# Retention plus bilinear feed-forward: another instruction order for the opening, query decay at the copy of the transposed queries, one state bank for both halves

## The chip, the cores and the metric

One NeuronCore of a Trainium2 chip runs the whole program. The metric is device time in microseconds (us) of one execution. Matmuls run on TensorE (PE), with separate weight loads (PEld); VectorE (DVE), ScalarE (ACT) and GpSimd (POOL) do element-wise work; SyncE (SP) mostly starts DMAs. ACT and POOL start some DMAs too. Each engine takes its instructions in the order in which they are written, and waits at an instruction whose data is not there.

## The reference, cut to what matters

```python
# q, k, v: (8 batches, 8 heads, 576 positions, 64), float32
scores = scale * q @ k.T                       # per head
Dmat   = where(rel >= 0, gamma[h] ** rel, 0)   # rel = query position - key position
att    = (scores * Dmat) @ v
x      = att.transpose(0, 2, 1, 3).reshape(4608, 512)
out    = ((x @ w_a) * (x @ w_b)) @ w_out       # 512 -> 1536 -> 512, float32
```

The decay `gamma ** (i - j)` is split into a factor of the query's position `i` (with `scale`; table `qs_o`) and one of the key's position `j` (table `vs`, multiplied into the values).

## The kernel before, in words

**The work as a whole.** The 4608 tokens are handled in feed-forward blocks of 512, 256, 256, and then 512 tokens (`blocks`). For a block, PE forms `pa = x @ w_a` and `pb = x @ w_b` for each of twelve slices F of 128 columns (lines 1398 and 1419), ACT copies `pa` to `ha` (L1412), DVE multiplies it with `pb` to `hT` (L1424), and PE forms rows `po` from `hT` and `w_out` (L933, L1445). Retention for later tokens is put between these matmuls, at moments counted in units of a 128x512 matmul: the list `todo` holds a unit and a function, and the loop at the end of the kernel calls a function at the first permitted point at or after its unit.

**The opening** is what comes before the first `pb`. It makes the retention of the first 256 tokens of batches 0 and 1, each as two steps of four heads: step 0 is batch 0 with heads 0-3, step 2 is batch 0 with heads 4-7, steps 1 and 3 are the same for batch 1. Steps 4 and 5 (batch 2, "the third") come later, inside the rows of the first feed-forward block. In a step (names and lines of the kernel before):

- loads of q, k and v, 256 KB each (`load_step`, L182): eleven of the twelve on SP's queue, step 0's k on ACT's;
- casts of q and k to bf16 (`cast_step`, L371), and values times key decay (`values_step`, L379 on ACT, L381 on DVE or POOL);
- PE transposes of q and k, four of 128x128 each (`transpose_step`, L389), copied from PSUM to `qkT` (L393);
- 16 score matmuls (`score_step`, L407), and one DVE instruction that multiplies 128x1024 scores with the causal mask (L415);
- 16 state matmuls, keys times values (L434), for the two halves a = 0, 1 of the 256 positions, into two PSUM tiles; ACT copies the first half to `state_after` in bf16 (L446, L467) and both halves to `own` and `second` (L450, L451, L469, L471), which are added later (`total_of`, L478, L481);
- two matmuls that take the state of the first half to the queries of the second (`step_states`, L504), and 16 of masked scores times values (`step_keys`, L520);
- `close_step` (L536, L541): DVE multiplies the 128x512 output in PSUM with the query decay `qs_o` and writes `x` in bf16.

The order is written out by hand (lines 1477 to 1554). Transposes and casts of steps 0, 2, 1 and 3 are started in that order; the masks are made in the order 0, 2, 1, 3. At the end stand `last_states` (states of steps 1 and 3, both halves, in one go), the outputs of 1 and 3, their closes, and then 16 matmuls of 128x256 for the first two slices of `pa` (`begin_with`, L922): slice F, contraction chunk c, token half m (m = 0 is batch 0, m = 1 is batch 1). Chunks c = 0, 1 of batch n come from its first step, c = 2, 3 from its second. `warm` issues matmuls whose result is not used (L1471), 19 in the opening.

The weights come by DMAs that POOL starts (L294, L296, L299), cast from float32 on the way: pieces of `WCOLS` slices for `w_a` and `w_b`, then three pieces of `w_out` (`wo_sb`). A one-row DMA into `gate` (L1550) makes SP's queue wait until the first piece of `w_out` has arrived; behind it stand the loads of steps 4 and 5 and of the later pairs.

**The third:** `early_casts` at unit 100, the cast of step 5's q at 112.1, `third_turn` (all 16 transposes and their copies) at 124, `third_states` at 128, `third_outputs` and `total_of(2)` at 136. The first block's `pa` and `pb` take 96 units; its rows begin there.

PSUM: the pool `ps_ffn` (tag "ab") has four banks that are handed round; `ps_sc` and `ps_o` hold one tile of two banks each.

Of the kernel before, what the change touches and what calls it, by code (L numbers as in the profile page):

```python
# [18 lines left out]
def kernel(  # L19
# [220 lines left out]
    qs_o = begin.tile([128, HP, 256], FP32)  # L240
    nc.vector.tensor_copy(qs_o[:, HP - 1],
                          idx_o.rearrange("p u k x -> p (u k x)"))
# [13 lines left out]
    def decays_next(step):  # L256
        if step == 0:
            nc.scalar.activation(later_half, lgp, AF.Exp, bias=0.0,
                                 scale=256.0)
        else:  # L260
            c = step - 1
            nc.scalar.mul(
                qs_1[:, c].rearrange("p (u x k) -> p u x k", u=2, k=2),
                qs_o[:, c].rearrange("p (u k x) -> p u x k", u=2, k=2),
                later_half[:, c:c + 1])

    def pair_tables(step):
# [6 lines left out]
        else:  # L274
            for h in (2 * step - 2, 2 * step - 1):
# [8 lines left out]
                for n in range(FIRST)]  # L284
    second = sum_pool.tile([128, FIRST, HP, 64], FP32, tag="sums",
                           name="second")
# [97 lines left out]
    def transpose_step(i, *ways):  # L384
        qkb, qkT = natural[STEPS[i]][0], transposed[STEPS[i]]
        tp = ps_ffn.tile([128, len(ways), 4, 128], BF16, tag="ab", name="tp")
        for to, (w, on) in enumerate(ways):
            for c in range(4):
                nc.tensor.transpose(tp[:, to, c, :],  # L389
                                    qkb[:, w, c * 128:c * 128 + 128],  # L390
                                    identity)
        for to, (w, on) in enumerate(ways):
            COPY[on](qkT[:, w], tp[:, to].rearrange("p c x -> p (c x)"))  # L393

# [26 lines left out]
    def state_step(i, rest=None):  # L421
        state_copies(i, state_products(i, [
            ps_ffn.tile([128, 2, 64], FP32, tag="ab", name=f"kv0{a}")
            for a in (0, 1)], set(QUADS)), rest)

    def state_products(i, kvs, fresh):
# [3 lines left out]
        for j in (0, 1):  # L430
            for kp in (0, 1):
                for a, r in QUADS:
                    e0 = kp * 256 + (2 * j + r) * 64
                    nc.tensor.matmul(kvs[a][half(r), j, :],  # L434
                                     qkb[half(a), 1, e0:e0 + 64],
                                     vb[half(a), e0:e0 + 64],
                                     start=(a, r) in fresh, stop=True,
                                     skip_group_check=True)
                    fresh.discard((a, r))
        return kvs  # L440

    def state_copies(i, kvs, rest=None):
        n, hh = STEPS[i]
        cs = slice(2 * hh, 2 * hh + 2)
        for r in (0, 1):
            nc.scalar.copy(state_after[half(r), n % 2, cs, half(r)],  # L446
                           kvs[0][half(r)])

        def keep():
            nc.scalar.copy(own_sums[n][:, cs], kvs[0])  # L450
            nc.scalar.copy(second[:, n, cs], kvs[1])  # L451

        if rest is None:
            keep()
        else:
            rest.append(keep)

    def last_states():

        own, later_half = kvs = [  # L460
            ps_ffn.tile([128, 2, 2, 64], FP32, tag="ab", name=f"kv1{a}")
            for a in (0, 1)]
        fresh = set(QUADS)
        for i in (1, 3):
            state_products(i, [kv[:, i // 2] for kv in kvs], fresh)
        for r in (0, 1):
            nc.scalar.copy(state_after[half(r), 1, :, half(r)],  # L467
                           own[half(r)].rearrange("p i j d -> p (i j) d"))
        nc.scalar.copy(own_sums[1],  # L469
                       own.rearrange("p i j d -> p (i j) d"))  # L470
        nc.scalar.copy(second[:, 1],  # L471
                       later_half.rearrange("p i j d -> p (i j) d"))

    def total_of(n):

        own = own_sums[n]
        if n < FIRST - 1:
            nc.gpsimd.tensor_tensor(own, own, second[:, n], op=ALU.add)  # L478
            nc.gpsimd.tensor_copy(own_states[n], own)
        else:  # L480
            nc.vector.tensor_tensor(own, own, second[:, n], op=ALU.add)  # L481
            nc.scalar.copy(own_states[n], own)
# [4 lines left out]
    def out_of(i, a):  # L487
        o = outputs[i]
        return o[a] if isinstance(o, list) else o[:, a]

    def open_step(i, place=None):
        if place is ps_ffn:
            outputs[i] = [ps_ffn.tile([128, 512], FP32, tag="ab",
                                      name=f"o0{a}") for a in (0, 1)]
        elif place is None:
# [32 lines left out]
    def close_step(i):  # L528
        n, hh = STEPS[i]
        cs = slice(2 * hh, 2 * hh + 2)  # L530
        x, by = x_of(256 * n, 256)[:, cs], qs_o[:, cs]
        o = outputs.pop(i)
        if isinstance(o, list):
            for a in (0, 1):
                at = slice(128 * a, 128 * a + 128)
                nc.vector.tensor_tensor(  # L536
                    x[:, :, at],
                    o[a][:, 0:256].rearrange("p (j s) -> p j s", j=2),
                    by[:, :, at], op=ALU.mult)
            return  # L540
        nc.vector.tensor_tensor(  # L541
            x.rearrange("p j (a s) -> p a j s", a=2),
            o[:, :, 0:256].rearrange("p a (j s) -> p a j s", j=2),
            by.rearrange("p j (a s) -> p a j s", a=2), op=ALU.mult)

    def output_step(i, place=None):
        open_step(i, place)
        step_states(i, True)
        step_keys(i, {0})
        close_step(i)  # L550

# [340 lines left out]
    WCOLS = [2, 3, 3, 4]  # L892
# [467 lines left out]
    BY_HALVES = [(256 * MIXED, F) for F in (8, 9, 10)]  # L1360
# [116 lines left out]
    warm(8, 512)  # L1477
    make_qs(qs_o, 0, 0, 256)
    for i in range(4):
        place_step(i)  # L1480
    cast_step(0, Q, "dve")
    cast_step(0, K, "dve")
    make_qs(qs_o, 1, 0, 256)
    transpose_step(0, (Q, "act"))
    transpose_step(0, (K, "dve"))
    values_step(0, 0, nc.scalar)
    values_step(0, 1, vector)
    make_qs(qs_o, 2, 0, 256)
    cast_step(2, Q, "pool")
    warm(2, 512)  # L1490
    score_step(0)
    warm(1, 512)
    state_step(0)
    transpose_step(2, (Q, "dve"))
    cast_step(2, K, "pool")
    cast_step(1, K, "pool")
    warm(2, 512)
    transpose_step(2, (K, "dve"))
    warm(2, 512)
    load_w(*pieces[0], "a")  # L1500
    cast_step(1, Q, "act")
    score_step(2)
    transpose_step(1, (K, "act"))
    output_step(0)
    transpose_step(1, (Q, "act"))
    values_step(2, 1, pool_)
    values_step(2, 0, pool_)
    make_qs(qs_o, 3, 0, 256)
    load_w(*pieces[0], "b")
    load_w(*pieces[1], "a")  # L1510
    warm(2, 512)
    cast_step(3, K, "dve")
    score_step(1)
    cast_step(3, Q, "act")
    rest = []
# [183 lines left out]
```

## Time and profile before

| | us |
|---|---|
| median of 3 runs (lowest to highest) | 314.4 (313.92 to 314.42) |
| profiled execution, its own time | 314.35 |
| its span (first to last instruction) | 312.6 |
| PE busy in the span | 303.2 (97%) |
| DVE / ACT / POOL busy | 226.3 / 155.6 / 203.5 |
| first `pb` matmul begins | 18.14 |
| rows of the first block begin | 37.13 |
| granted TensorE clock | 1.0 throughout |

Times of instructions are counted from the start of the span. A line of a timeline gives start, duration, engine, line, operation, written tile <- read tiles, shape and count; in square brackets stands how long the engine had been idle and who released it. Instructions of one engine overlap a little, so consecutive starts lie closer together than the durations say. The chain of waits goes back from the last instruction, at each step to what released it; its lines are start, length, engine and tile.

### The profile page before, as it was taken

How to read it: one execution, taken by the hardware profiler on the slowest of the kernel's cores; microseconds unless marked ns; L12 is line 12 of the kernel's file. 1: busy time of each engine (PE TensorE's matmuls, PEld its weight loads, DVE VectorE, ACT ScalarE, POOL GpSimd, SP SyncE). 2: the span in 40 equal slices, each digit the busy share in tenths (PEclk: the TensorE clock that was granted, in tenths of full speed). 3: DMA queues.
4: the chain of work that ended last, by engine and by line, in shares of the span. 5: the costliest groups of instructions: out<-in, count | busy, mean ns of one | idle time of the engine just before them, and what ended most of it. 6: DMA issues, size and time to landing. Idle time of an engine off the chain costs nothing.

```text
span 312.6 us, 9645 instructions
## 1 busy us (share of the span) xinstructions
PE 303.2 (97%) x3922; PEld 199.1 (64%) x3955; DVE 226.3 (72%) x450; ACT 155.6 (50%) x351; POOL 203.5 (65%) x290
## 2 busy tenths in 40 slices
PE   8899999999999999999999999999999999999995
PEld 3554457868544554557874787468746875687774
DVE  5845337767747796779878886888679968877873
ACT  6755335626434554455456546544635454335530
POOL 4990088585996599763799769985999350035413
PEclk9999999999999999999999999999999999999999
DMA  7999999999978999999999487838703020013004
GB/s 230 265 199 206 265 252 204 175 198 221 204 152 219 219 227 189 248 247 248 201 285 220 89 203 186 198 78 183 219 2 70 24 113 2 2 52 86 1 2 134
DMA packets 144797, 50.97 MB, mean 163 GB/s; under 512 B 126576, under 2 KB 141680, under 8 KB 144752
## 3 DMA queue, kind: packets, MB, share of 16 engines
q1 hardware_dynamic: 138272, 45.10, 63.6%
q0 software_dynamic: 5808, 4.72, 9.7%
q8 instruction: 31, 0.51, 0.7%
q10 hardware_dynamic: 672, 0.52, 0.5%
q14 instruction: 14, 0.11, 0.1%
HBM read 37.75 MB, written 9.44 MB: 151 GB/s over the span
## 4 chain that ended last, share of the span: by engine, by line
PE 91%; DVE 2%; DMA 2%; issue 2%; ACT 1%; SPq 1%; POOL 0%; DVEq 0%; ACTq 0%
PE m L1047 16%; PE pb L1419 13%; PE pa L1398 12%; PE pb L1284 9%; PE pa L1284 9%; PE po L1445 8%; PE lm L1227 7%; PE ls L1227 3%; PE la L1227 2%; PE po L933 2%; DMA kf<-in_k_dram 2%; PE sc L735 2%; PE o L763 1%; PE kv L664 1%; PE o L776 1%
## 5 line engine op out<-in xcount | busy, mean ns | idle before, releaser
L1424 DVE TENSOR_TENSOR hT<-ha,pb 128x512 bf16<-128x512 bf16 (+1 forms) x60 | 34.7, 579 | 32.9 <-PE pb L1419 27.4
L1419 PE MATMUL pb<-xT,wb_sb 128*128 128x512 bf16 (+1 forms) x237 | 49.9, 336 | 0.3
L1071 POOL TENSOR_TENSOR osb<-crossed,straight 128x256 f32<-128x256 f32 x24 | 17.5, 755 | 47.4 <-ACT crossed L1059 47.4
L1398 PE MATMUL pa<-xT,wa_sb 128*128 128x512 bf16 (+1 forms) x238 | 47.6, 326 | 0.5 <-issue 0.3
L1412 ACT CAST ha<-pa 128x512 bf16<-128x512 f32 (+1 forms) x60 | 29.7, 499 | 34.3 <-PE pa L1398 31.9
L1419 PEld LDWEIGHTS <-wb_sb 128*128 128x128 bf16 x240 | 23.4, 98 | 17.7 <-issue 0.3
L1398 PEld LDWEIGHTS <-wa_sb 128*128 128x128 bf16 x244 | 23.3, 98 | 16.6 <-DVE sums L691 0.2
L616 POOL TENSOR_TENSOR vb<-vf,vs 128x512 bf16<-128x512 f32 x30 | 31.6, 1072 | 1.7 <-PE pa L1398 0.6
L1284 PE MATMUL pb<-xT,wb_sb 128*128 128x512 bf16 x125 | 32.1, 379 | 0.2
L1284 PE MATMUL pa<-xT,wa_sb 128*128 128x512 bf16 x119 | 31.4, 379 | 0.7 <-issue 0.3
L579 POOL TENSOR_TENSOR qkb<-qf,qs 64x512 bf16<-64x512 f32 x24 | 24.9, 1052 | 10.3 <-DMA qf<-in_q_dram 6.9
L1047 PEld LDWEIGHTS <-hT 128*128 128x128 bf16 x288 | 28.1, 98 | 5.0 <-DVE hT L981 0.5
L1294 ACT CAST ha<-pa 128x512 bf16<-128x512 f32 x32 | 18.7, 584 | 24.8 <-PE pa L1284 24.8
L1297 DVE TENSOR_TENSOR hT<-ha,pb 128x512 bf16<-128x512 bf16 x32 | 21.9, 684 | 10.2 <-PE pb L1284 8.1
L609 POOL CAST qkb<-kf 64x256 bf16<-64x256 f32 x60 | 27.4, 484 | 1.5
L1445 PE MATMUL po<-wo_sb,hT 128*128 128x512 bf16 x113 | 26.7, 379 | 0.8 <-issue 0.6
L584 POOL TENSOR_TENSOR qkb<-qf,qs 64x512 bf16<-64x512 f32 x24 | 26.4, 1121 | 0.7
L1047 PE MATMUL m<-wo_sums,hsum 128*128 128x256 bf16 x216 | 25.7, 273 | 0.0
L981 DVE TENSOR_TENSOR hsum<-hT 128x512 bf16<-128x512 bf16 (+2 forms) x51 | 23.5, 493 | 0.5
L605 POOL CAST qkb<-kf 64x512 bf16<-64x512 f32 x30 | 20.1, 670 | 5.0 <-DMA kf<-in_k_dram 3.6
L1047 PEld LDWEIGHTS <-hsum 128*128 128x128 bf16 x216 | 21.1, 98 | 2.5
L1284 PEld LDWEIGHTS <-wb_sb 128*128 128x128 bf16 x128 | 12.3, 98 | 14.3
(159 smaller groups left out, 583.0 us busy)
## 6 DMA issues: line engine op xcount, KB each, us to landing
qf<-in_q_dram SPq DMA_DIRECT2D x32, 256.0 KB, 4.4
vf<-in_v_dram SPq DMA_DIRECT2D x32, 256.0 KB, 4.3
kf<-in_k_dram SPq DMA_DIRECT2D x31, 256.0 KB, 4.3
out_dram<-osb SPq DMA_DIRECT2D x9, 512.0 KB, 3.8
out_dram<-osb SPq DMA_DIRECT2D x22, 128.0 KB, 2.9
wo_sb<-in_moe_w_out_dram POOLq DMA_DIRECT2D x3, 512.0 KB, 15.5
out_dram<-osb SPq DMA_DIRECT2D x6, 256.0 KB, 3.8
qf<-in_q_dram SPq DMA_DIRECT2D x8, 128.0 KB, 3.2
```

The costliest lines, as they stand in the source:

```text
L579: nc.gpsimd.tensor_tensor(per_head(qkb[0:64, Q])[:, hs], per_head(t[0:64])[:, hs], by[0:64, hs].unsqueeze(2).to_broadcast([64, H, D]), op= ...
L584: nc.gpsimd.tensor_tensor(per_head(qkb[64:128, Q])[:, 1 - r::2], per_head(t[64:128])[:, r::2], by[64:128, r::2].unsqueeze(2).to_broadcast( ...
L609: nc.gpsimd.tensor_copy(to[:, :, 1 - r], fro[:, :, r])
L616: nc.gpsimd.tensor_tensor(vb[:, e].rearrange("p (h d) -> p h d", d=D), t[:, e].rearrange("p (h d) -> p h d", d=D), decay[:, at], op=ALU.mult)
L1047: nc.tensor.matmul(to, rows, cols, start=(begins and p == 0), stop=True, skip_group_check=True)
L1227: nc.tensor.matmul(to[:, m], w[:, c], x[:, c], start=(way in (1, 2, 5) and m == c == 0), stop=True, skip_group_check=True)
L1284: nc.tensor.matmul(p1, w[:, c, F * 128:F * 128 + 128], xT[:, c], start=(c == 0), stop=(c == NC - 1))
L1398: nc.tensor.matmul(pa[:, at:at + width], wa_sb[:, c, fs], xT[:, c, at:at + width], start=(c == at == 0), stop=(c == NC - 1), skip_group_ch ...
L1412: nc.scalar.copy(ha[:, 0:n], pa[:, 0:n])
L1419: nc.tensor.matmul(pb[:, 0:n], wb_sb[:, c, fs], xT[:, c], start=(c == 0), stop=(c == NC - 1))
L1424: nc.vector.tensor_tensor(hT[:, F, 0:n], has[F][:, 0:n], pb[:, 0:n], op=ALU.mult)
L1445: nc.tensor.matmul(po, hT[:, F, u * 128:(u + 1) * 128], wo_sb[:, F], start=(F == 0), stop=(F == NF - 1))
```

## The change

Eight edits; the loads, tables and helper functions first, then the new order.

```diff
-    for i, which in ((0, Q), (0, K), (0, V), (2, Q), (2, K), (1, K),
-                     (1, Q), (2, V), (3, K), (3, Q), (1, V), (3, V)):
+    for i, which in ((0, Q), (0, K), (2, Q), (0, V), (2, K), (1, Q), (3, Q), (2, V), (1, K), (3, K), (1, V), (3, V)):
...
-    def make_qs(t, c, s0, s1):
-        nc.scalar.activation(t[:, c, s0:s1], t[:, HP - 1, s0:s1], AF.Exp,
+    def make_qs(c):
+        nc.scalar.activation(by_pair(c), idx_f, AF.Exp,
                              bias=biasq[:, 0:1], scale=lgp[:, c:c + 1])
...
+    def states_from(i, kv, a, fresh):
...
     def total_of(n):
         own = own_sums[n]
-        if n < FIRST - 1:
-            nc.gpsimd.tensor_tensor(own, own, second[:, n], op=ALU.add)
-            nc.gpsimd.tensor_copy(own_states[n], own)
-        else:
-            nc.vector.tensor_tensor(own, own, second[:, n], op=ALU.add)
-            nc.scalar.copy(own_states[n], own)
+        (nc.gpsimd.tensor_copy if n < FIRST - 1 else nc.scalar.copy)(
+            own_states[n], own)
...
-    def close_step(i):
+    def close_half(i, j, on):
         n, hh = STEPS[i]
...
+        COPY[on](x_of(256 * n, 256)[:, 2 * hh + j].rearrange(
+            "p (a s) -> p a s", a=2), outputs[i][:, :, 128 * j:128 * j + 128])
...
-    WCOLS = [2, 3, 3, 4]
+    WCOLS = [2, 2, 4, 4]
...
-    BY_HALVES = [(256 * MIXED, F) for F in (8, 9, 10)]
+    BY_HALVES = [(1024, 4)] + [
+        (256 * MIXED, F) for F in (8, 9, 10)]
...
+    def turn_out(i, w, on):
+        tp = tps.pop((i, w)).rearrange("p c x -> p (c x)")
+        if w == Q:
+            nc.vector.tensor_tensor(transposed[STEPS[i]][:, w], tp,
+                                    qs_o[:, STEPS[i][1]], op=ALU.mult)
+        else:
+            COPY[on](transposed[STEPS[i]][:, w], tp)
```

`states_from` issues the 8 state matmuls of one half a; both halves now go into one PSUM tile, `kv`. `by_pair(c)` is a view of the table `qs_o`, which is now laid out as the transposed queries are; `idx_f` holds the positions. `turn_in` issues the four transposes of one operand of a step. `form_states(i, a)` calls `states_from`; `states_out` copies to `state_after` (two ACT instructions of 64 partitions) or to `own`. `scores_of` and `mask_of` are the two halves of `score_step`. `firsts(m, c...)` issues `begin_with` for the first two slices. A number in `warm` counts matmuls; 14 stand in the new opening.

The new order of the opening, which takes the place of lines 1477 to 1544 (several calls are put on one line here, and calls that only reserve PSUM are left out):

```diff
+    warm(8, 512); make_qs(0)
+    cast_step(2, Q, "pool"); cast_step(0, Q, "dve"); make_qs(3)
+    values_step(0, 0, pool_); cast_step(0, K, "dve")
+    turn_in(0, Q); warm(1, 512); make_qs(1); make_qs(2)
+    turn_in(0, K); turn_in(2, Q); turn_out(0, Q, "dve")
+    values_step(0, 1, vector); turn_out(0, K, "act"); warm(1, 512)
+    cast_step(1, Q, "pool"); scores_of(0, "o"); warm(1, 512)
+    cast_step(2, K, "act"); load_w(*pieces[0], "a")
+    turn_out(2, Q, "dve"); form_states(0, 0); states_out(0, "after", "act")
+    turn_in(2, K); step_states(0, True); turn_in(1, Q)
+    values_step(2, 1, pool_); mask_of(0); step_keys(0, {0})
+    turn_out(2, K, "dve"); cast_step(3, Q, "act"); close_half(0, 0, "act")
+    scores_of(2, "o"); close_half(0, 1, "act"); form_states(0, 1)
+    warm(1, 512); states_out(0, "own", "act"); values_step(2, 0, pool_)
+    warm(1, 512); turn_out(1, Q, "dve"); turn_in(3, Q)
+    cast_step(1, K, "act"); load_w(*pieces[0], "b"); load_w(*pieces[1], "a")
+    turn_in(1, K); form_states(2, 0); cast_step(3, K, "act")
+    states_out(2, "after", "act"); mask_of(2); turn_out(3, Q, "dve")
+    turn_in(3, K); turn_out(3, K, "act"); step_keys(2, {0, 1})
+    step_states(2, False); turn_out(1, K, "dve"); scores_of(1, "o")
+    close_half(2, 0, "act"); close_half(2, 1, "act"); warm(1, 512)
+    values_step(1, 1, pool_); values_step(1, 0, vector)
+    form_states(2, 1); states_out(2, "own", "act"); mask_of(1)
+    form_states(1, 0); scores_of(3, "sc"); values_step(3, 0, pool_)
+    values_step(3, 1, pool_); states_out(1, "after", "act"); mask_of(3)
+    firsts(0, 0); step_keys(1, {0, 1}); step_states(1, False)
+    form_states(3, 0); firsts(0, 1); states_out(3, "after", "act")
+    firsts(0, 2); firsts(0, 3); close_half(1, 1, "dve")
+    step_keys(3, {0, 1}); step_states(3, False); close_half(1, 0, "dve")
+    form_states(1, 1); close_half(3, 0, "act"); load_w(*pieces[1], "b")
+    form_states(3, 1); firsts(1, 1); close_half(3, 1, "act")
+    firsts(1, 0); states_out("last", "own", "act")
```

The four matmuls of chunks 2 and 3 of batch 1 stay where they were, at the head of the first block. Then the loads of the third, and its places:

```diff
-    nc.sync.dma_start(gate, wo_sb[0:1, 3, 0:64])
-    for i, which in ((4, Q), (4, K), (4, V), (5, Q), (5, K), (5, V)):
-        load_step(*STEPS[i], which)
+    for i, arrived in ((4, wb_sb[0:1, 0, DFF - 64:]), (5, wo_sb[0:1, 3, 0:64])):
+        nc.sync.dma_start(gate, arrived)
+        for which in (Q, K, V):
+            load_step(*STEPS[i], which)
...
-            (124, third_turn, ()), (128, third_states, ()),
-            (136, third_outputs, ())]
+            (116.5, third_turn, ()), (126, third_states, ()),
+            (134, third_outputs, ())]
```

`third_states` now forms only the first half's states, `third_outputs` the second half's, and the third's closes are two plain copies on ACT (step 4) and two on DVE (step 5). Its transposed queries are multiplied by `qs_o` on DVE, its keys copied on ACT.

More of the change, by code (lines that the diff above doesn't have):

```diff
@@ new lines, in states_out @@
+    def states_out(i, to, on):
+        n, hh = (1, 0) if i == "last" else STEPS[i]
+        kv = kvs_of["last" if n else i][0]
+        if n and i != "last":
+            kv = kv[:, hh:hh + 1]
+        cs = slice(0, HP) if i == "last" else slice(2 * hh, 2 * hh + 2)
+        for hp in (half(0), half(1)) if to == "after" else (slice(0, 128),):
+            COPY[on](state_after[hp, n, cs, hp] if to == "after" else
+                     own_sums[n][:, cs],
+                     kv[hp].rearrange("p i j d -> p (i j) d"))
@@ L1535 @@
[L1535 to L1544 removed]
+    turn_in(1, K)
+    form_states(2, 0)
+    cast_step(3, K, "act")
+    states_out(2, "after", "act")
+    mask_of(2)
+    turn_out(3, Q, "dve")
+    turn_in(3, K)
+    turn_out(3, K, "act")
```

310 lines of the change are left out of this document (163 added, 147 removed).

## The prediction

> **What bounds the kernel now.** The page comes first: PE is busy for 97% of the span at full granted clock, so time can be won only where PE waits or does work that is not needed.
>
> ```profile
> span 312.6 us, 9645 instructions
> PE 303.2 (97%) x3922; PEld 199.1 (64%) x3955; DVE 226.3 (72%) x450; ACT 155.6 (50%) x351; POOL 203.5 (65%) x290
> PEclk9999999999999999999999999999999999999999
> ```
>
> Of the 9.4 us in which PE is idle, some 4 us lie before the first `pb`; and its busy time there holds 19 unused matmuls. The chain of waits, asked for the first 19 us, says what the opening runs on.
>
> ```profile
> 2.96 4.92 DMA kf<-in_k_dram
> 7.94 0.62 POOL qkb L371
> 8.59 0.40 PE tp L389 x4
> ...
> 13.15 0.58 ACT qkT L393
> 13.73 0.17 ACT own L450
> 13.90 0.17 ACT second L451
> 14.07 0.96 ACT vb L379 x4
> 15.07 0.30 PE kv L434 x7
> 15.37 0.35 ACT state_after L467
> 15.73 0.38 ACT state_after L467
> 16.15 0.40 PE o L504 x4
> 16.55 1.75 PE pa L922 x16
> ```
>
> A load, a cast, transposes, a copy; at the end ACT alone: two copies that nobody needs yet (L450, L451), four instructions for step 3's values, then the state copies, and only then PE with all sixteen first `pa` matmuls. From 18.14 on, the timeline of PE has no gap worth naming until 45.9: whatever the opening ends earlier, PE can take over in full, if weights and the third's data keep up. The timeline of DVE gives the four masks:
>
> ```profile
> 7.24 1.23 DVE L415 TENSOR_TENSOR sT<-sc,mask_s 128x1024 bf16<-128x1024 f32 x1 [0.47 <-POOL qkb L371]
> 9.96 1.22 DVE L415 TENSOR_TENSOR sT<-sc,mask_s 128x1024 bf16<-128x1024 f32 x1 [0.53 <-PE sc L407]
> 12.17 1.22 DVE L415 TENSOR_TENSOR sT<-sc,mask_s 128x1024 bf16<-128x1024 f32 x1
> 14.32 1.23 DVE L415 TENSOR_TENSOR sT<-sc,mask_s 128x1024 bf16<-128x1024 f32 x1 [0.53 <-PE sc L407]
> ```
>
> The last mask ends at 15.55 and `pb` begins at 18.14: 2.6 us of tail.
>
> **The loads.** Issue time plus time to landing, from the DMA view, gives for the places on SP's queue: 4.3, 5.4, 6.3, (7.0, no landing recorded, put between), 7.9, 8.6, 9.5, 10.2, 10.9, 11.7, 12.5. The sizes stay, so I give the new order the same places: q of 2 at 5.4 (was 6.3), v of 0 at 6.3, k of 2 at 7.0, q of 1 at 7.9, q of 3 at 8.6, v of 2 at 9.5, k of 1 at 10.2 (was 7.9), k of 3 at 10.9 (was 10.2), v of 1 and 3 at 11.7 and 12.5 as before.
>
> **The opening, laid out from rows.** Durations: DVE cast 0.43, copy of a transposed operand 0.42 on DVE and 0.58 on ACT, ACT cast 0.61, POOL cast 0.61 to 0.87, POOL values 0.61 per half, four transposes 0.40, 16 score matmuls 0.42, mask 1.22. The new turn of q is a 128x512 product with float32, which the trace has only as the close (L541, 0.68, a float32 source). Bounds: 0.42, the plain copy, and 0.68; I take 0.68, same width and same kind of table.
>
> DVE's sum hardly changes: four turns of q and two copies of k in place of four copies, +1.9; a half of values, +0.4; a cast less, -0.4; closes (L541 three times, L536 twice) become two plain copies of 0.42, -2.0. ACT takes six plain closes of at most 0.37 (L469's row), and gives up four own/second copies and two times four instructions of values (0.96).
>
> - Mask 0: q's turn 5.6 to 6.3, values at 6.3 when v lands, turn of 2's q to 7.4; mask 7.4 to 8.6. Before 7.24: 0.15 late.
> - Mask 2: k of 2 copied 8.6 to 9.0, its scores 9.35 to 9.75 behind step 0's keys; turn of 1's q between; mask 9.8 to 11.05 (was 9.96).
> - Mask 1, third as before: k of 3 lands 10.9, ACT casts to 11.55, transposes to 11.95, step 2's keys and states (0.45) to 12.4, scores to 12.85; mask to 14.05. Before 12.17: 0.7 late.
> - Mask 3: its scores need 3's k (copied 12.55), step 2's PSUM freed (ACT closes 12.95) and the states of step 1 before them (POOL values 13.05): scores to 13.65. So the mask follows mask 1 at once, 14.05 to 15.27 (was 14.32 to 15.55).
> - Meanwhile PE does the 8 `pa` matmuls of batch 0 (0.88), step 1's keys and the states of 3 (POOL values end 14.2, as before). The first `pa` matmul needs the first weight piece: issued 8.50, 5.3 to landing, 13.8; PE is there at 13.7, nothing lost.
> - Tail: keys of 3 from 15.35 (0.36), its states (0.1), state matmuls of the second halves (0.25), 8 `pa` matmuls of batch 1 (1.75/16 x 8 = 0.88): `pb` at 16.9. ACT closes step 3 by 16.5, before PE asks for it.
>
> **18.14 - 16.9: 1.25 us won**, nearly all of it in the tail. Five fewer `warm` matmuls (0.21 each) lie in gaps: counted at nothing; the granted clock reads 1.00 in every 2 us of the opening. The query table's four exponentials (0.54 each) end near 5.5, just ahead of the first turn; if late, 0.1 at most, hidden behind mask 0's slack.
>
> **Weights.** Before, they land at 13.8, 15.5, 18.0, 19.95, 22.0, 24.0, 26.5, 29.05, and `w_out` at 31.6, 34.1, 36.7: 0.2 MB/us. Smaller second pieces land at some 17.2 and 19.2, the 512 KB third ones at 21.8 and 24.4. PE asks at 16.9 plus multiples of 1.73: 18.6, 20.4, then 22.1 for the third `w_a` piece: 0.3 to spare (in the trace before: 3). Bounds: 0 to 0.4 lost.
>
> **The third.** Its turn stands one edge (4 matmuls, 0.86 us) earlier, and all of PE 1.25: the transposes of 5's k, the last four of the sixteen that begin at 43.17 and take 0.89, come from 43.84 to 43.84 - 2.1 = 41.75. POOL casts this k at 40.84 after waiting for it; SP, with four loads in flight, is held at exactly this load (2.68 us long, from 34.55). The two gates open SP's queue at 29 instead of 31.6, but bytes come only behind `w_out`: before, q of 4 issued at 32.29 landed at 37.9, 1.2 after `w_out`'s last piece. So I count on no earlier landing, and 0 to 0.7 later (two more pieces of half width, the first of which took 1.7 instead of 1.3): cast done 41.45 to 42.2, PE waits 0 to 0.4. I take 0.25 for both waits. What POOL and DVE lose in additions (L478, L481: 0.72 twice, 1.1) and DVE in the third's closes is off PE's path: nothing. The halved slice in the block at 1024 costs 0.01.
>
> **Sum**: 314.35 - 1.25 + 0.25 = 313.35, on the scale of the median (314.40) **313.4**.
>
> **Rivals.**
> - *The opening's chain does not shorten*: k of 1 and 3 now are the last keys and ACT casts both, behind closes. Every 0.1 us late moves masks 1 and 3. If the two land or are cast 0.9 late, `pb` begins at 17.8: 314.0 to 314.2. For it: that cast is what sets mask 1 in my layout, and mask 1 is already later than before. Against: ACT idles for over 2 us in my layout before them. 0.19, a quarter of it slower than before.
> - *The third is the new wall*: 5's k cast at 42.9, `pb`'s gain given back: 314.2. For it: that cast did wait for its load before. Against: the load would have to land 1.45 later than before. 0.10.
> - *Slower: the earlier loads take bandwidth from `w_out`.* Opened at 29, step 4's bytes could flow from 31.5 beside the 1.05 MB then left. At half rate these take 10.2 us, to 41.7; PE needs the last piece 16 matmuls into its rows, 40.6 - 1.25 = 39.35, and waits 2.35: 315.5. It decides from a landing past 40.6. Against: the last piece came 2.55 us after the one before, full rate, with three loads issued beside it. 0.08. The Trainium skill, "DMA: Bandwidth & Descriptors", section "Queues, rings and completion order", says that each DMA engine goes round its queues packet by packet; by that rule the queues would share and this rival would hold, and the row above speaks against it.
> - *More*: PE-bound opening, nothing lost later, 312.4 to 312.7. 0.05.
> - That the edit does not do what it says: the instruction order shows as many state matmuls, five `warm` fewer, four halves more. Not counted.
>
> **Chances.** Forecast 0.58 (312.7 to 313.75), the others as given. Of a median some 0.2% (0.6 us) can be told from no change. Faster: 0.58 + 0.05 = 0.63; same: three quarters of 0.19 and 0.10 = 0.24; slower: 0.05 + 0.08 = 0.13. The range reaches 312.6 to 314.9, which leaves out part of the last two.
>
> **What would show it.** First `pb` at 16.9 (right within 0.3), masks 1 and 3 back to back, eight `pa` matmuls before the last mask ends; PE's wait at the third's transposes for POOL or ACT under 0.5; the last `w_out` piece by 38. It is wrong if DVE is idle between masks 1 and 3, if a turn of q takes much over 0.7, or if PE waits at a weight piece.

## The result and the profile after

The changed kernel takes 315.24 us (median of 22 executions, 314.62 to 316.70), the kernel before 314.52 us beside it (22 executions, 313.84 to 317.17): the ratio is 1.0027, with a 95% interval of 1.0016 to 1.0037. It is slower by some 0.85 us, where I forecast 1 us less, and it lies above my range. The profiled execution took 315.02 us.

The page of the changed kernel, the same three lines as for the kernel before:

```profile
span 313.2 us, 9664 instructions
PE 305.7 (98%) x3954; PEld 199.2 (64%) x3954; DVE 223.6 (71%) x448; ACT 155.8 (50%) x345; POOL 202.1 (65%) x288
PEclk9999999999999999999999999999999999999999
```

DVE and POOL have less work, ACT the same, and PE is as full as before. (PE's two sums cannot be compared closely: the profile of the kernel before holds 33 matmuls fewer than weight loads, 3922 and 3955, this one none.) What counts is where PE's work lies and how long it takes. The masks on the timeline of DVE:

```profile
7.33 1.22 DVE L1457 TENSOR_TENSOR sT<-sc,mask_s 128x1024 bf16<-128x1024 f32 x1
9.62 1.21 DVE L1457 TENSOR_TENSOR sT<-sc,mask_s 128x1024 bf16<-128x1024 f32 x1
12.94 2.36 DVE L1457 TENSOR_TENSOR sT<-sc,mask_s 128x1024 bf16<-128x1024 f32 x2 [0.85 <-PE sc L1446]
```

Masks 0, 2, and then 1 and 3 back to back: within 0.2 us of my layout, the last one ends at 15.30 (I had 15.27). The chain of waits up to the first `pb` (start, length, engine, tile) has changed all the same:

```profile
2.96 4.90 DMA qf<-in_q_dram
...
7.91 0.55 POOL qkb L373
8.46 5.74 DMA wa_sb<-in_moe_w_a_dram
...
14.25 0.39 PE pa L842 x2
14.65 0.35 PE o L465 x16
14.99 0.22 PE o L449 x2
15.21 0.24 PE kv L420 x8
15.45 0.76 PE pa L842 x6
16.21 0.35 PE o L465 x16
16.56 0.22 PE o L449 x2
16.78 0.37 PE kv L420 x16
17.15 0.98 PE pa L842 x8
```

No mask and no ACT copy is in it any more. It runs over the first weight piece, for which PE stands 0.55 us at the first `pa`, and from there over PE alone. The first `pb` begins at 17.96, 0.18 earlier than in the profile of before instead of 1.25.

The second place is the third (timeline of PE). Before:

```profile
45.02 0.42 PE L407 MATMUL sc<-qkT 64*64 64x128 bf16 x16
45.27 0.29 PE L434 MATMUL kv<-vb,qkb 64*64 64x64 bf16 x16
45.41 0.42 PE L407 MATMUL sc<-qkT 64*64 64x128 bf16 x16
45.65 0.29 PE L434 MATMUL kv<-vb,qkb 64*64 64x64 bf16 x16
...
47.62 0.39 PE L504 MATMUL o<-qkT,state_after 128*128 128x128 bf16 x4
```

and after:

```profile
45.00 0.42 PE L398 MATMUL sc<-qkT 64*64 64x128 bf16 x16
...
45.82 1.90 PE L1366 MATMUL po<-wo_sb,hT 128*128 128x512 bf16 x8
47.66 0.44 PE L420 MATMUL kv<-vb,qkb 64*64 64x64 bf16 x16
48.03 0.40 PE L449 MATMUL o<-qkT,state_after 128*128 128x128 bf16 x4
```

From the first scores to the first output matmul it takes 3.03 us instead of 2.60. The 16 state matmuls of the second halves now stand alone ahead of the outputs and take 0.37. Half of the state matmuls have left the place behind the scores, and that place has hardly become shorter.

### The profile page after: what moved, and what is told of

It reads as the page before. It is cut to its first block, busy times and chain, and to the rows that moved or that the text cites. A ratio compares the mean times of both kernels' runs of the same rounds, so it can differ in the third digit from the quotient of the medians.

```text
span 313.2 us, 9664 instructions
## 1 busy us (share of the span) xinstructions
PE 305.7 (98%) x3954; PEld 199.2 (64%) x3954; DVE 223.6 (71%) x448; ACT 155.8 (50%) x345; POOL 202.1 (65%) x288
## 4 chain that ended last, share of the span: by engine, by line
PE 92%; DMA 3%; DVE 2%; SPq 1%; issue 1%; ACT 0%; POOL 0%; DVEq 0%; ACTq 0%
PE m L967 16%; PE pb L1340 13%; PE pa L1319 12%; PE pa L1204 9%; PE pb L1204 9%; PE po L1366 8%; PE lm L1147 7%; PE ls L1147 3%; DMA wa_sb<-in_moe_w_a_dram 2%; PE la L1147 2%; PE po L853 2%; PE sc L655 2%; DMA qf<-in_q_dram 2%; PE o L683 1%; PE kv L584 1%; PE o L696 1%
## 5 line engine op out<-in xcount | busy, mean ns | idle before, releaser
L1319 PE MATMUL pa<-xT,wa_sb 128*128 128x256 bf16 (+1 forms) x248 | 48.3, 324 | 0.0
L1204 PE MATMUL pa<-xT,wa_sb 128*128 128x512 bf16 x128 | 32.9, 379 | 0.0
L529 POOL CAST qkb<-kf 64x256 bf16<-64x256 f32 x60 | 28.2, 498 | 1.5
L1366 PE MATMUL po<-wo_sb,hT 128*128 128x512 bf16 x120 | 27.6, 380 | 0.0
L901 DVE TENSOR_TENSOR hsum<-hT 128x512 bf16<-128x512 bf16 (+2 forms) x51 | 23.6, 496 | 0.5
```

The lines of the kernel that those rows point to most:

```text
L529: nc.gpsimd.tensor_copy(to[:, :, 1 - r], fro[:, :, r])
L1204: nc.tensor.matmul(p1, w[:, c, F * 128:F * 128 + 128], xT[:, c], start=(c == 0), stop=(c == NC - 1))
L1319: nc.tensor.matmul(pa[:, at:at + width], wa_sb[:, c, fs], xT[:, c, at:at + width], start=(c == at == 0), stop=(c == NC - 1), skip_group_ch ...
L1366: nc.tensor.matmul(po, hT[:, F, u * 128:(u + 1) * 128], wo_sb[:, F], start=(F == 0), stop=(F == NF - 1))
```

## The experiments

Each kernel below was run on its own, its ratio is to the kernel before. "Rows" is the start of the first block's first `po`; "third" is from there to the first output matmul of the third; "later" is from that matmul to the last instruction; all from the profiled execution. "Wait" is PE's idle time at the first `pa` for the first weight piece.

| kernel | first `pa` (wait) | rows | third | later | ratio (95% interval) |
|---|---|---|---|---|---|
| before | 16.39 | 37.13 | 10.49 | 265.0 | 1 |
| c0, before again | 16.35 | 37.09 | 10.49 | 265.1 | 1.0007 (0.9999 to 1.0016) |
| b3, before + pieces, halved slice | 16.17 | 36.91 | 10.49 | 265.2 | 0.9999 (0.9990 to 1.0008) |
| b5, before + values on DVE | 16.05 | 36.79 | 10.48 | 265.2 | 1.0005 (0.9986 to 1.0024) |
| b1, before + one bank | 15.78 | 36.52 | 10.95 | 264.9 | 0.9999 (0.9988 to 1.0009) |
| b1r, the same again | 16.04 | 36.78 | 10.95 | 265.4 | 1.0027 (1.0017 to 1.0037) |
| b6, before + whole changed third | 16.20 | 36.94 | 10.97 | 265.4 | 1.0026 (1.0014 to 1.0038) |
| after | 14.25 (0.55) | 36.96 | 11.07 | 265.2 | 1.0027 (1.0016 to 1.0037) |
| c1, after again | 14.42 (0.31) | 37.12 | 10.98 | 265.8 | 1.0031 (1.0019 to 1.0043) |
| e3g, one gate | 14.21 (0.58) | 36.91 | 10.98 | 265.2 | 1.0026 (1.0015 to 1.0037) |
| e4, plain turn | 14.29 (0.51) | 36.99 | 11.26 | 265.6 | 1.0024 (1.0012 to 1.0035) |
| e6, no halved slice | 14.71 (1.21) | 37.41 | 10.97 | 265.1 | 1.0036 (1.0021 to 1.0051) |
| e2, two banks | 14.49 (0.65) | 37.20 | 10.51 | 265.8 | 1.0016 (0.9999 to 1.0032) |
| e23, third as before | 14.67 (1.19) | 37.37 | 10.87 | 265.5 | 1.0032 (1.0020 to 1.0045) |
| e5, weights early | 14.29 | 37.93 | 11.40 | 265.7 | 1.0048 (1.0027 to 1.0068) |
| e1, keys first | 15.03 | 36.82 | 10.98 | 265.3 | 1.0032 (1.0012 to 1.0052) |
| e123, keys first, third as before | 14.90 | 36.69 | 10.87 | 265.4 | 1.0019 (1.0010 to 1.0027) |
| e12, keys first, two banks | 14.84 | 36.63 | 10.55 | 265.3 | 1.0009 (0.9999 to 1.0020) |
| e12g, e12 and one gate | 15.01 | 36.80 | 10.52 | 266.0 | 1.0015 (1.0004 to 1.0025) |
| f1, e12 and step 0 ahead | 16.11 | 37.90 | 10.51 | 265.8 | 1.0045 (1.0029 to 1.0061) |

My theories: **W**, the opening's gain is lost at the first `pa`, which waits for its weights; **H**, state matmuls of one half at a time, in one bank, take PE longer; the rivals are **D**, DVE's longer turn of q, and **G**, the third's earlier turn and its gates. In e2, "two banks" means the arrangement of the kernel before: both halves interleaved, over four quarters of the array and two banks.

**e1: keys ahead of the first `pa`.**

```diff
     mask_of(3)
-    firsts(0, 0)
     step_keys(1, {0, 1})
     step_states(1, False)
     form_states(3, 0)
+    firsts(0, 0)
     firsts(0, 1)
```

> The changed kernel with one edit: the two first pa matmuls, which wait for the first weight piece, are issued behind step 1's keys and states and the state matmuls of step 3, not ahead of them. Theory W (in the opening PE stands 0.55 us for the first weight piece with ready work behind it, and from there on PE alone is the bound): the idle time before the first pa falls under 0.15, the first pb begins at 17.5 to 17.65 instead of 17.96, and the time falls by 0.3 to 0.45 us, to a ratio near 1.0015. Rival D (the query decay at the turn on DVE makes the masks late and these set the end): first pb moves by less than 0.1, ratio 1.0025 or more.

The first `pb` came 0.13 earlier than in the changed kernel's profile, not 0.3 to 0.4. PE waits nearly as long as before, but for another cause, as the timeline of PE shows:

```profile
14.22 0.42 PE L465 MATMUL o<-sT,vb 64*64 64x128 bf16 x16 [0.51 <-DVE sT L1457]
14.57 0.29 PE L449 MATMUL o<-qkT,state_after 128*128 128x128 bf16 x2
14.79 0.31 PE L420 MATMUL kv<-vb,qkb 64*64 64x64 bf16 x8
15.03 1.05 PE L842 MATMUL pa<-xT,wa_sb 128*128 128x256 bf16 x8
```

The keys wait for mask 1, which ends at 14.17. In the changed kernel's profile the piece landed at 14.21, at the same moment as the mask, so there PE would have had nothing to do until 14.2 in either order. In e1, however, the piece, which POOL issued at 8.46 as in the changed kernel, took 6.24 us to land instead of 5.74 and was there only at 14.7. So e1 does not speak against W: PE did the keys while it would have stood for the piece. In e6, whose order is unchanged and whose piece landed at 14.66, rows begin 0.59 later than in e1. The time, 1.0032 with a wide interval, shows no gain.

**e2: two banks again in the third.**

```diff
     def third_states():
...
-        states_from(4, kv[:, 0], 0, fresh)
+        both_halves(4, [kv[:, 0], kv_b[:, 0]], fresh)
         score_step(5, ps_o[0], "o")
-        states_from(5, kv[:, 1], 0, fresh)
+        both_halves(5, [kv[:, 1], kv_b[:, 1]], fresh)
...
+        nc.vector.tensor_tensor(
+            own_sums[2], own_sums[2],
+            kv_b.rearrange("p i j d -> p (i j) d"), op=ALU.add)
...
     def third_outputs():
-        for i in (4, 5):
-            states_from(i, kv[:, i - 4], 1, set())
```

> The changed kernel with one edit: in the third the state matmuls of both halves are issued together again, over all four quadrants of the array and into two PSUM banks, which DVE adds; the opening stays as changed. Theory H (state matmuls of one half use two quadrants only, 23 ns each, and cost PE some 0.33 us more in the third): first scores of the third as in the changed kernel, its rows resume at 48.5 to 48.65 instead of 48.93, time 0.25 to 0.4 us less, ratio near 1.0017. Rival G (the third is dear because its turn comes early and stands for step 5's k): rows resume within 0.1 of 48.93, ratio 1.0025 or more.

The third falls from 11.07 to 10.51, what it took before. The timeline of PE in e2:

```profile
45.15 0.42 PE L398 MATMUL sc<-qkT 64*64 64x128 bf16 x16
45.39 0.29 PE L1617 MATMUL kv<-vb,qkb 64*64 64x64 bf16 x16
45.52 0.40 PE L398 MATMUL sc<-qkT 64*64 64x128 bf16 x16
45.74 0.29 PE L1617 MATMUL kv<-vb,qkb 64*64 64x64 bf16 x16
45.97 1.90 PE L1366 MATMUL po<-wo_sb,hT 128*128 128x512 bf16 x8
47.71 0.39 PE L449 MATMUL o<-qkT,state_after 128*128 128x128 bf16 x4
```

From the scores to `po` it is 0.82 us with all 32 state matmuls, exactly as long as the changed kernel takes with 16 (45.00 to 45.82); the other 16 are then saved. The starts of the state matmuls say why: 16 of both halves, in two banks, lie within 0.10 us, and 8 of one half, in one bank, as well. H holds, and G is not needed. What the experiment does not separate is the bank from the parts of the array: one half uses two of the four quarters that both halves use together.

**b1 and b1r: that part alone in the kernel before** (the opposite edit: `kv4` in one tile, second halves in `third_outputs`).

> The kernel before with one part of the change alone: in the third the states of the first half are made into one bank, those of the second half behind the scores in the same bank, no addition; opening, weights and times of the third as before. Theory H: PE pays 0.3 to 0.4 us more in the third, rows resume at 48.8 to 48.95 instead of 48.51, ratio 1.0009 to 1.0013. Rival G (the early turn or the gate costs it): rows resume within 0.1 of 48.51 and the ratio is 1.0000 to 1.0004.

> The kernel of b1 (before, with the third's states in one bank) a second time. Theory H: the stage from first scores to the outputs takes 3.06 again instead of 2.60, and the ratio of both measurements together lies at 1.0005 to 1.0015. If it is 1.0000 again, the 0.46 of the stage does not reach the end of the program in this kernel, and the third is not what made the changed kernel slower.

The stage is longer by 0.46 in both. The times disagree: 0.9999 and 1.0027, on two different chips, each beside the kernel before. Their mean of 1.0013 fits the stage's 0.46 (1.0015); either alone would have misled.

**e4: q turned by a plain copy** (`if w == Q and i >= 4` in `turn_out`).

> The changed kernel with the q of steps 0 to 3 copied from PSUM without the decay (0.42 instead of 0.69 us on DVE, four times): it leaves out the query decay of the first 512 tokens. Theory W: masks come up to 0.3 us earlier, but the first pa waits for the same weight piece at 14.2, so the first pb begins within 0.1 of 17.96 and the ratio stays at 1.0025 or more. Rival D: masks 1 and 3 come 0.5 or more earlier and the first pb with them, ratio 1.0012 or less.

The kernel leaves out the query decay of the first 512 tokens. Mask 1 begins at 13.01 instead of 12.94, and the first `pa` is at 14.29 as without the edit: the longer turn is not what the opening waits for, and D falls.

**e5: first weight piece earlier, all eight `pa` of batch 0 ahead of the keys.**

```diff
     warm(1, 512)
+    load_w(*pieces[0], "a")
     cast_step(1, Q, "pool")
...
-    load_w(*pieces[0], "a")
     turn_out(2, Q, "dve")
...
     firsts(0, 0)
+    firsts(0, 1)
+    firsts(0, 2)
+    firsts(0, 3)
     step_keys(1, {0, 1})
```

> The changed kernel with two edits in the opening: POOL starts the DMA of the first weight piece ahead of the cast of 1's q instead of behind it, and all eight pa matmuls of batch 0 stand ahead of step 1's keys. e1 showed that moving the keys ahead of the wait changes nothing, since they wait for mask 1, which ends at the same 14.2 as the piece lands. Theory W2 (two walls at one moment, 14.2; PE is idle from 13.6 and has 3.7 us of work from there): the piece lands near 13.0, the eight matmuls fill the idle stretch, the first pb begins at 17.3 to 17.5 instead of 17.96. Rival D (the masks set the end): the cast of 1's q and, with the weights' bytes beside them, the last keys come later, masks 1 and 3 move by 0.3 or more and pb stays within 0.15 of 17.96 or is later.

Rows come 0.97 later, not 0.5 earlier. Some 0.5 of this is not the edit's: mask 0 begins at 7.85 instead of 7.33, since PE came to its full speed later in this execution and the v of step 0 landed 0.5 later, at 6.86, before the piece was issued. The piece was issued at 7.73 instead of 8.46. Behind it the v of step 3 landed at 14.38 instead of 12.44, POOL, which waited for it, issued the later pieces later, and one of them kept PE waiting 0.52 in the first block. The ratio of 1.0048 beside 1.0027 says that the edit costs time; that the weights take bandwidth from the loads fits, but is not shown.

**e3g: one gate**, on `w_out`, as before.

> The changed kernel with one edit: one gate, on the first w_out piece, ahead of all six loads of the third, as in the kernel before; the third's times and everything else as changed. Theory G2 (the second gate, which stands behind the first one's own landing, holds SP's queue to 35.4, so that the loads of all later pairs start 1.2 us later, POOL's casts with them, and this is the 0.2 to 0.8 us that the changed kernel and its three variants lose between 50 us and the end): first pair load issued at 38 instead of 39.35, the time from the end of the third to the last instruction 264.0 to 264.15 instead of 264.27 to 264.9, and the wait for step 5's k gone; total 0.3 to 0.6 less. Rival H alone: rows resume at most 0.15 earlier, the rest as it was, total within 0.2.

**e23: the whole third as before** (two banks, 124, 128, 136, one gate).

> The changed kernel with the whole third as before: two banks and four quadrants, turn, states and outputs at 124, 128 and 136, one gate on w_out; opening, weights and the rest as changed. Theory H with G2: from the first row to the resumed rows 11.35 to 11.45 us as in the kernel before (11.38) instead of 11.97, rest 264.0 to 264.2, so only the opening's gain of 0.2 is left: ratio 0.9990 to 1.0000. Rival, that something else of the change costs the later time (the halved slice at 1024, the pool's tiles): rest stays at 264.3 or more and the ratio at 1.0008 or more.

**e6: without the halved slice.**

> The changed kernel without the halved slice in the block at 1024 (the block is as in the kernel before). My count for that edit was 0.01 us. Theory: nothing changes, time within 0.15 of the changed kernel and rest 264.2 to 264.9. Rival: the halved slice shifts the phase of DVE and POOL in the blocks behind it and is what the later loss comes from; then the rest falls to 264.0 to 264.15 and the time by 0.2 to 0.5.

All three stay at 1.0026 to 1.0036. The gates matter little: e3g has 0.09 less in the third, but so has c1, which is the changed kernel unedited, and nothing less later. e23 misses too: its third takes 10.87, 0.38 longer than before, since the scores now wait for q's turn with the decay on DVE and for the copy of k on ACT, which starts behind it; the earlier turn of the change is what hides that. e23 and e6 show W in its full form, with the piece landing at 14.62 and 14.66 (e23, timeline of PE):

```profile
14.67 0.39 PE L842 MATMUL pa<-xT,wa_sb 128*128 128x256 bf16 x2 [1.19 <-DMA wa_sb<-in_moe_w_a_dram]
```

Mask 1 had ended at 13.93 here; keys that were ready stood some 0.7 us behind the weights.

**c0 and c1: both kernels again, and e12: keys first with two banks; e12g: one gate as well.**

> The kernel before itself, a second time: how far the opening's length varies by itself. In the two profiles of it (the second with the third in one bank) its rows begin at 37.13 and 36.52. Theory W (its first pa comes 2.6 us after the first weight piece, so a late piece costs it nothing): rows at 36.5 to 37.2, the first pa follows the last mask's keys without a wait for a DMA; ratio 1.0000 with an interval of some 0.001 to either side.

> The changed kernel itself, a second time. Theory W: PE stands at the first pa for the first weight piece by as much as that piece lands late, which in the runs so far was 14.2 to 14.7 (0.5 to 1.2 us of idle time), so rows begin at 36.9 to 37.4 and the piece's landing and the rows move together; ratio 1.0020 to 1.0035. Rival D (DVE's masks set the end): rows move with the masks and not with the piece.

> The changed kernel with e1's order (step 1's keys ahead of the first pa) and e2's third (two banks, four quadrants). W with H: when the piece lands later than mask 1 ends, the keys fill 0.8 us of the wait, so rows begin at 36.4 to 36.9 with no wait for the weight DMA, the third takes 11.35 to 11.45, and the ratio is 0.9995 to 1.0015. If neither mattered for the median: 1.0025 or more.

> The kernel of e12 with the single gate on w_out of the kernel before as well. If the second gate's late loads cost anything that e3g's 1.0026 hid, the ratio is 0.0005 or more below that of e12 and the time behind the third falls to 264.1; otherwise it equals e12 within the interval. It is also the candidate for a version as fast as the kernel before: 0.9990 to 1.0010.

In all six profiles with the changed opening, rows begin 22.70 or 22.71 after the first `pa`, and 22.75 after the landing of the first weight piece, which varies from 14.16 to 14.66: the piece moves everything. With the old opening the piece lands just as variably (13.61 to 14.66), and nothing waits for it, since the first `pa` stands at 15.78 or later. e12 is the best version of the changed kernel, 314.58 us beside 314.60 for the kernel before, with a ratio of 1.0009 and 1 inside the interval: not to be told from equal, and not better. One gate instead of two adds nothing (e12g).

**e123: the changed opening alone, keys first; b3: weight pieces and halved slice alone; b5: half of step 3's values on DVE, in the kernel before.**

> The changed kernel with step 1's keys ahead of the first pa and the whole third as before (two banks, 124, 128, 136, one gate): of the change, only the opening, the weight pieces and the halved slice are left. W: rows begin at 36.6 to 36.8 with no wait for the weight DMA; the third takes 11.4 to 11.8 (q's turn with the decay is 0.27 longer twice on DVE); ratio 1.0000 to 1.0015. If the new opening by itself makes the kernel slower, 1.0020 or more.

> The kernel before with the weight pieces 2, 2, 4, 4 and the halved slice in the block at 1024, nothing else. My prediction counted 0 to 0.4 for the pieces (PE waits at the third w_a piece) and 0.01 for the slice. As no kernel with these pieces showed a wait behind the first piece: ratio 1.0000 within 0.001, from the third to the end 264.0 to 264.25. Rival: these two edits are what the changed kernel loses behind the third; then that time is 264.3 or more and the ratio 1.0010 or more.

> The kernel before with one edit: the first half of step 3's values is made on DVE, in its idle 0.5 us ahead of mask 3, not by four ACT instructions (0.96). If ACT's chain (own, second, values, state copies) sets the opening's end as the chain of waits says, the last state matmuls begin at 14.3 instead of 15.07 and the keys of step 3, behind mask 3, become the end: first pa at 16.1 to 16.2 instead of 16.4, ratio 0.9990 to 0.9997. Rival: mask 3 is pushed back by the values and nothing is won, 1.0000 or more.

b3 is 0.9999: the two edits cost nothing. e123 is still slower, 0.0012 of its 0.0019 by the third's 0.38. In b5 the first `pa` comes 2.89 us after mask 1's end instead of 3.00: ACT's chain did set the end, but mask 3's keys stand 0.1 behind it. The ratio (1.0005, 0.9986 to 1.0024) cannot show so small a gain.

**b6: the whole changed third in the kernel before. f1: e12 with step 0's scores and mask ahead of 2's q.**

> The kernel before with the changed third alone: one bank, second halves behind the scores, turn, states and outputs at 116.5, 126 and 134, two gates; q and k copied plainly, opening and weights as before. H with the small part for the turn: from the first row to the resumed rows 11.85 to 12.0 us (before 11.38), ratio of 1.0015 to 1.0025. If the third is not what costs: 1.0008 or less.

> The kernel of e12 (keys first, two banks) with step 0's scores ahead of the transposes of 2's q on PE, and its mask ahead of the turn of 2's q on DVE. Rival D (DVE's late start moves the whole opening): mask 0 begins at 6.6 to 6.9 instead of 7.3 to 7.6, mask 1 ends 0.3 to 0.5 earlier, rows at 36.3, ratio 0.9985 to 1.0000. My layout (mask 1 hangs on 3's k, which lands at 10.9 and is cast by ACT to 11.5): mask 0 earlier, mask 1's end within 0.1 of 14.0, rows 36.6 to 36.8, ratio within 0.0007 of that of e12.

b6 gives 1.0026, as much as the whole change. f1 does not decide about D, since mask 0 did not come earlier: PE was still at half speed, and ACT's copy of k came later. Against e12, mask 2 comes 0.8 later and mask 1 1.3 later; the second part of the loss is at the values on DVE (DVE's timeline, and POOL's beside it):

```profile
12.36 1.74 DVE L383 TENSOR_TENSOR vb<-vf,vs 128x256 bf16<-128x256 f32 x1
```

```profile
12.04 1.77 POOL L383 TENSOR_TENSOR vb<-vf,vs 128x256 bf16<-128x256 f32 x3
```

The same instruction took 0.41 in the changed kernel, where it began at 11.68, ahead of POOL's at 12.26, and 0.88 in e12, at 11.54, ahead of POOL's at 12.04.

## Why the prediction was wrong

**The masks, the turn of q, the landings on SP's queue: right.** q's turn took 0.69 (I took 0.68); mask 3 ended 0.03 from where I had it. That it was so close is partly luck: mask 1 ended 0.12 late and mask 3 began before that end, and in the six profiles with this opening mask 3 ends between 15.06 and 15.70. The step "the opening, laid out from rows" holds up to the last mask.

**The tail: wrong, 1.06 of the 1.25.** The step "PE is there at 13.7, nothing lost; keys of 3 from 15.35; `pb` at 16.9" failed in three ways, from the chain above. PE began at 14.25, not 13.7 (0.55): the piece took 5.74 to land, not 5.3, and step 1's keys, which stand behind it, could not have filled the wait, since mask 1 ended at 14.17. The 5.3 came from one profile, near the shortest: with the old opening the piece takes 5.26 to 6.25 in seven profiles. Work that I let fit between 13.7 and 15.35 (1.65) takes 1.89. I had given a price there only to the eight `pa` matmuls, 0.88; in two groups, with a change of matmul shape behind each, they take 1.08, and step 1's keys take 0.35, its two `step_states` matmuls 0.22, the eight state matmuls of step 3 0.24. Behind it I counted 1.59 and it takes 1.82: two `step_states` matmuls are 0.22, not 0.1, and 16 state matmuls 0.37, not 0.25. From 16.94, the sum of my terms, 0.55 + 0.24 + 0.23 leads to 17.96. I had made PE the bound and then not summed PE. Nor were there "some 4 us" of idle PE ahead of the first `pb`: in the profile of before PE is busy for 15.36 of these 18.14 us, which leaves 2.8, and 1.53 of that lies ahead of its first instruction.

**The point it was counted from: wrong by another 0.23.** I took 18.14, one execution's start of `pb`. Six profiles with that opening (before, c0, b1, b1r, b3, b6) have their rows at 36.52 to 37.13, 36.90 in the mean; the one that I read was the latest (the section on the hardware shows what that goes with). The six with the changed opening (after, c1, e2, e3g, e6, e23) have 36.91 to 37.41, 37.16 in the mean. The opening that was to win 1.25 loses 0.26. With the keys first (e1, e12, e12g, e123) the mean is 36.74.

**The third: the missed term.** I wrote that the instruction order "shows as many state matmuls" and counted no cost for putting both halves into one bank. The number is the same, the price is not. The second halves, 16 matmuls in one bank, now stand alone: 0.25 us from the first start to the last, another 0.12 until the first output matmul starts (together the 0.37), and some 0.09 are lost ahead of them, behind `po` (0.31 from the last `po` start to the first of them, 0.22 to the first output matmul in e2). That is 0.46. What went from the place behind the scores saves nothing: 32 over two banks take no more there than 16 in one. The stage grows by 0.46 (b1, b1r), and b6 with the rest of the third by 0.48. In time: e2, e12 and e12g with two banks have a mean ratio of 1.0013, the kernels with the changed third and the changed opening (after, c1, e1, e3g, e6) 1.0030: 0.0017, or 0.5 us, where each ratio has an interval of 0.001 to 0.002 to either side. The Trainium skill, "TensorEngine Tiling (Array Packing)", section "Gotcha 1: PSUM Pressure", says that different row tiles cannot access the same PSUM bank at the same time. The two halves are two row tiles, so by that rule they cannot run side by side in one bank. The rows show what it costs to run them apart; no run issues both at once into one bank, so the rule itself is not tested here. I did not weigh it.

**The third's other waits: size right, by luck.** The transposes took 1.21 instead of 1.06 in the profile, a wait of 0.15 for the casts of 5's q and k (0.06 in c1, for q alone), where I took 0.25 for this and the weights. But the cast of 5's k, which I had done at 41.45 to 42.2, ended at 42.9, against 41.45 before (timeline of POOL):

```profile
42.28 0.61 POOL L373 CAST qkb<-kf 128x512 bf16<-128x512 f32 x1 [0.33 <-DMA kf<-in_k_dram]
```

The gates did not open the queue early for step 5: the second one was issued at 35.40, when the DMA of the first had landed, and 5's q behind it at 35.97, against 34.00 before. In the nine profiles of the changed opening with two gates (f1 among them) this cast ends between 42.08 and 44.19. Had `pb` come at 16.9, 1.06 earlier, PE would have asked for this k near 41.75 and waited some 1.1 us (an estimate from these starts). That is the rival "the third is the new wall", which I gave 0.10; the late opening hid it.

PE waited for no weight piece after the first, and b3 is 0.9999. The rival of `w_out` sharing its bandwidth did not cost anything: PE waits for no DMA between 18 us and the third. But its mechanism is not refuted. The last piece of `w_out` landed at 39.26, 3.63 after the one before it, past the 38 that I had named as a sign; before, it was 36.68 and 2.56. With one gate in the changed kernel (e3g, e12g, e23, e123) the distance is 2.67 to 2.70, with two gates 3.44 or more. It is no proof, since c0, the kernel before again, has 3.86. The rival nearest to what happened is the first, "the opening's chain does not shorten", but by other means than the casts that I named.

**What stays open.** On the means, opening (0.26) and third (0.5) give 0.76 of the 0.85 to 0.97 that the ratios 1.0027 and 1.0031 say. "Later" is 265.0 to 265.2 in the four profiles with the third of before and its opening, and 264.9 to 266.0, 265.5 in the mean, in the others. In the profiles this comes in steps of 0.1 to 0.5 at various places, different ones in two executions of the same kernel (after and c1); one is behind 143 us in c1, where two bf16 operations on DVE (L901) take 2.75 instead of 1.53 beside POOL's multiplications. Without the second gate (e3g, 265.2), without the halved slice (e6, 265.1) and with the weight pieces and the halved slice alone (b3, 265.2) it is much as in the changed kernel's own first profile (265.2), so none of these is shown to be its cause, and no run settles it. Why b1 and b1r differ by 0.0028 stays open as well.

## What to carry to other kernels

Once an opening is bound by one engine, add up that engine's instructions group by group, and put behind a wait only what needs it: work that is ready must not stand behind a DMA. Equal numbers of matmuls are not equal time: ask which banks and which parts of the array work together before and after, and whether a group now stands alone. A gain of under 1 us should be counted from several profiles of the kernel before, since one start alone can be off by 0.6 and the landing of one transfer by 1.

## What was not expected of the hardware

**PE's start at half speed, at no fixed time.** The same opening runs from 4.9 us at two speeds. Before, and b1 (timeline of PE):

```profile
4.92 1.06 PE L389 MATMUL tp<-identity,qkb 128*128 128x128 bf16 x8
5.77 1.00 PE L1471 MATMUL w<-ones 128*128 128x512 bf16 x2
6.70 0.42 PE L407 MATMUL sc<-qkT 64*64 64x128 bf16 x16
```

```profile
4.78 0.70 PE L389 MATMUL tp<-identity,qkb 128*128 128x128 bf16 x8
5.32 0.59 PE L1470 MATMUL w<-ones 128*128 128x512 bf16 x2
6.00 0.42 PE L407 MATMUL sc<-qkT 64*64 64x128 bf16 x16
```

Eight transposes take 0.85 to the next start in one execution and 0.54 in the other, and step 0's scores begin 0.7 apart, while the granted clock reads 1.00 in both. In the six profiles with the old opening these scores begin at 6.00 to 6.70, and rows follow them by 30.4 to 30.6; the profile that I counted from was the latest in both. In the changed order the scores stand behind the transposes of 2's q, for which POOL's cast ends near 6.1. They begin at 6.67 to 6.74 in the eight profiles in which PE had its full speed by the transposes of step 0's k (after, c1, e12 and e23 among them), and at 6.95 to 7.31 in the four in which it had not (e1, e2, e5, e12g): an early speed-up wins nothing there, and a late one costs. The Trainium skill, "TensorE: Matmul & The Clock Gate", section "What's actually happening", says that the clock opens after a busy window that runs freely and is not aligned with the kernel's start; the spread here agrees.

**DVE behind POOL.** The multiplication of 0.41 that took 1.74 (f1) has two operands in SBUF, as has POOL's beside it. The Trainium skill, "SBUF — State Buffer", section "Who interferes with whom", says that a DVE instruction with two SBUF inputs contends with a GpSimd instruction that reads SBUF. f1's 1.74 agrees: DVE's began at 12.36, during the first of POOL's three, and ended at 14.11, 0.3 after the third. Its 0.88 in e12, where it began first, shows that the order alone does not save it. This makes the values a poor choice for DVE while POOL makes values too (b5's took 0.78 and ended 0.3 after POOL's).
